# Four x tiles through one DMA queue, and a new emission order for the head of an adaLN attention block

## The chip, the cores and the metric

The kernel runs on one core of a Trainium2 chip. The metric is the device time of one execution in microseconds (us), as a median over several executions. A profiled execution also has a span, from its first to its last recorded instruction, which is a little shorter than its device time. The engines are PE (TensorE: matmuls and transposes), DVE (VectorE), ACT (ScalarE), POOL (GpSimd) and SP (SyncE, here only an issuer of DMAs). Each runs its own instruction stream strictly in order; semaphores tie the streams together.

## The reference, cut to what matters

```python
B, N, D = (2, 256, 1152)
def reference(x, c, wqkv, wo, w_mod):
    mod = (_silu(c) @ w_mod).reshape(B, 6, 1, D)
    shift_a, scale_a, gate_a, shift_m, scale_m, gate_m = [mod[:, i] for i in range(6)]
    h = _layernorm(x, axis=-1) * (1 + scale_a) + shift_a
    q, k, v = split(h @ wqkv)                  # D columns each
    p = _softmax(q @ k.T * D ** (-0.5), axis=-1)
    a = (p @ v) @ wo
    return x + gate_a * a
```

All tensors are bf16. There are 512 tokens (two batches of 256), and the weights are 1152 x 3456 (wqkv), 1152 x 1152 (wo) and 1152 x 6912 (w_mod, of which only the shift, scale and gate thirds of the first half are read).

## The kernel before

**Tiling.** The 512 tokens are four x tiles of 128 tokens: tiles 0 and 1 are batch 0, tiles 2 and 3 are batch 1. The model dimension is nine chunks of 128. Projections keep the activations transposed (feature on partitions): `xnT_sb` holds x transposed, `h0T_sb` (the same buffer as `pvT_sb`) holds it centred and scaled.

**Stages.** The head loads x and c, transposes x on PE, subtracts the token mean and multiplies by 1 + scale. The key projection then accumulates over the nine chunks in seven PSUM banks at once ("ka", `NA` = 7), chunk by chunk as the weights land. Afterwards come two more key blocks, the queries with the shift added, values, scores, softmax, the gate, P times V, the output projection and the stores.

**Loads.** SP issues nearly all loads. First come x tiles 2, 0 and 1, and then the scale columns of w_mod ("s", four groups, into `wm_sb`) alternating with key weight rows ("w", into `wq_sb`), in the order of `LOADS`. Tile 3 and c are issued by ACT, in front of its activation table load. L280 is an x tile, L284 a group of scale columns, L291 a piece of wqkv.

**Emission order.** `ORDER` is a list, written out, of the head's work items; each item appends its instructions to the stream of its engine. So the list fixes the order within each engine, and data dependencies do the rest. `_Prog.op` derives the waits: a read waits for the last writer, and accesses to one PSUM bank by two different engines wait for each other in the order of the list.

The items that the change touches, with their engines and lines:

- `sum i` (ACT, L387): row sums of x tile i, 1.16 us each plus an accumulator read; `sq i` (ACT, L398): row sums of squares. `nmT i` (PE, L363) transposes the sums of a tile into PSUM bank 6. `nmu2` (POOL, L520) turns the sum of tile 2 into a mean that `sq 2` needs.
- `mean 3` (PE, L392): the mean of tile 3 by nine matmuls with ones, from its transposed chunks, also into bank 6.
- `xT i part` (PE, L348): transposes of tile i, part 0 four chunks and part 1 five. `out i part E` (L338 on DVE, L340 on ACT) copies them from PSUM to `xnT_sb`. Tiles 1 and 2 share PSUM banks.
- `nm b E` (L373 on ACT, L371 on DVE): the negative means of batch b from bank 6 to `nm_sb`. `cen cc tiles` (DVE, L382) adds them to a chunk.
- `smm g` (PE, L426): the scale vector of group g, needs load s g; `sev g` (DVE, L456) adds 1 to it. `scale cc tiles E` (L476 on DVE, L480 on ACT) writes `h0T_sb`.
- `early k` and `late k` (PE, L491): the key matmuls of chunk k for five and two of the seven banks.
- `e1`, `d1`, `rc`, `scT`: the small chain ACT, POOL, DVE, POOL that makes silu(c).

After `ORDER`, a fixed program follows: group 2 (chunks 4 and 5) is centred and scaled, then chunks 4 to 8 of the keys run on PE, with `smm 3` (L435, needs the fourth scale load, s3) in front of the last four matmuls of chunk 5.

Of the kernel before, what the change touches and what calls it, by code (L numbers as in the profile page):

```python
# [12 lines left out]
AC = mybir.EngineType.Activation  # L13
POOL = mybir.EngineType.Pool
SP = mybir.EngineType.SP
# [6 lines left out]
class _Prog:  # L22
# [12 lines left out]
    def op(self, eng, fn, r=(), w=(), dma=False, extra=()):  # L35
        o = _Op()
        o.eng, o.fn, o.dma = eng, fn, dma
        o.sem = o.val = None
        o.inc = False
        deps = set(extra)  # L40
        for k in r:
            if k[0] == "ps":
                continue
            p = self.last_w.get(k)
            if p is not None and not (p.eng == eng == PE):
                deps.add(p)
            self.readers.setdefault(k, []).append(o)
        for k in w:
            if k[0] == "ps":
                continue  # L50
            for q in self.readers.get(k, ()):
                if q is not o and (q.dma or dma or q.eng != eng):
                    deps.add(q)
            p = self.last_w.get(k)
            if p is not None and p is not o and not (p.eng == eng == PE):
                deps.add(p)
            self.readers[k] = [o] if k in r else []
            self.last_w[k] = o
        for k in set(r) | set(w):
            if k[0] != "ps":  # L60
                continue
            accesses = self.bank.setdefault(k, {})
            for e, q in accesses.items():
                if e != eng:
                    deps.add(q)
            accesses[eng] = o
        deps.discard(o)
        o.deps = deps
        self.ops.append(o)
        return o  # L70
# [73 lines left out]
D = 1152  # L144
# [22 lines left out]
CUT = ("w", "qa", 8)  # L167
WARM = 5
ORDER = [
    ('cT',), ('warm', 4), ('cTo',), ('sum', 2), ('nmT', 2), ('e1',), ('xT', 2, 0), ('d1',), ('xT', 0, 0),  # L170
    ('xT', 3, 0), ('rc',), ('xT', 3, 1), ('xT', 2, 1), ('sum', 0), ('nmT', 0), ('out', 2, 0, 'D'), ('nmu2',),
    ('out', 3, 0, 'D'), ('scT',), ('sum', 1), ('xT', 1, 0), ('out', 3, 1, 'D'), ('mean', 3), ('out', 0, 0, 'D'),
    ('out', 2, 1, 'D'), ('nm', 1, 'A'), ('xT', 0, 1), ('xT', 1, 1), ('nmT', 1), ('out', 1, 0, 'D'),
    ('out', 1, 1, 'A'), ('cen', 0, (2, 3), 'D'), ('smm', 0), ('cen', 0, (0, 1), 'D'), ('nm', 0, 'A'),
    ('out', 0, 1, 'A'), ('sev', 0), ('scale', 0, (2, 3), 'D'), ('early', 0, (2, 3)), ('scale', 0, (0, 1), 'D'),
    ('cen', 1, (0, 1, 2, 3), 'D'), ('scale', 1, (0, 1), 'D'), ('cen', 3, (0, 1, 2, 3), 'D'),
    ('cen', 2, (0, 1, 2, 3), 'D'), ('early', 0, (0, 1)), ('late', 0), ('scale', 1, (2, 3), 'A'), ('late', 1),
    ('smm', 1), ('sev', 1), ('sum', 3), ('scale', 2, (2, 3), 'A'), ('scale', 2, (0, 1), 'D'), ('early', 1),
    ('sq', 0), ('scale', 3, (0, 1), 'D'), ('late', 2), ('sq', 1), ('scale', 3, (2, 3), 'D'), ('late', 3),
    ('early', 2), ('smm', 2), ('early', 3),  # L180
]

# [1 line left out]
def bass_standalone__dit_adaln_block__diffusion_kernel(  # L184
    nc: bass.Bass,
    x: bass.AP,
    c: bass.AP,
    wqkv: bass.AP,
    wo: bass.AP,
    w_mod: bass.AP,  # L190
    out: bass.AP,
):
    with ExitStack() as es:
        _build(nc, es, x, c, wqkv, wo, w_mod, out)


def _build(nc, es, x, c, wqkv, wo, w_mod, out):
# [81 lines left out]
    def load_x(eng, i):  # L279
        op(eng, lambda e: e.dma_start(x_sb[:, i, :], x_pi[:, i, :]), w=[("x", i)], dma=True)  # L280
# [12 lines left out]

    op(AC, lambda e: e.dma_start(c_sb[:, :], c[:, :]), w=[("c",)], dma=True)
    load_x(SP, 2)
    load_x(AC, 3)
    op(AC, lambda a: a.preload_act_table_set("natural_log_exp_and_others"))
    for t in LOADS:
        pg.tag = ("ld",) + t
# [15 lines left out]
    for k0 in range(0, DC, 3):  # L315
# [7 lines left out]
        out=ident[:, :], in_=ident[:, :], compare_op=ALU.not_equal, fill=1.0,  # L323
# [188 lines left out]
    early, late = tuple(range(EARLY)), tuple(range(EARLY, NA))  # L512
# [332 lines left out]
```

## Time and profile before

| | us |
|---|---|
| median of 4 runs | 97.68 (97.53 to 98.66) |
| profiled execution, its own time | 97.53 |
| profiled execution, its span | 95.7 |
| PE busy | 91.1 |
| DVE, ACT busy | 50.7, 32.1 |

The granted TensorE clock is full over the whole span. When each early load was issued and when it had landed (issue start plus the trace's time from issue to landing):

| load | KB | issued by, at | to landing | landed at |
|---|---|---|---|---|
| x tile 2 | 288 | SP 0.74 | 2.9 | 3.6 |
| x tile 0 | 288 | SP 1.19 | 4.0 | 5.2 |
| x tile 3 | 288 | ACT 1.30 | 5.0 | 6.3 |
| x tile 1 | 288 | SP 1.66 | 4.9 | 6.6 |
| s0 | 576 | SP 2.12 | 6.7 | 8.8 |
| w chunk 0 | 224 | SP 2.60 | 6.8 | 9.4 |
| w chunk 1 | 224 | SP 3.93 | 6.2 | 10.1 |
| s1 | 576 | SP 4.40 | 7.7 | 12.1 |
| w chunks 2, 3 | 448 | SP 5.01 | 8.3 | 13.3 |
| s2 | 576 | SP 7.66 | 7.7 | 15.4 |
| s3 | 864 | SP 10.96 | 8.6 | 19.6 |

To read the profile: a wait is charged to whatever released it, and an engine's idle time costs nothing unless the chain of work that ends last runs through it.

### The profile page before, as it was taken

Reading aid. Unit: us, or ns where it says so; the run is one execution under the profiler, and the core shown is the slowest. Engines: PE = TensorE matmul, PEld = TensorE weight load, DVE = VectorE, ACT = ScalarE, POOL = GpSimd, SP = SyncE. Lnnn points to the kernel's source line nnn. Section 1 sums busy time; section 2 is a strip of 40 time slices with the busy share of each in tenths; the row PEclk is TensorE's granted clock in tenths of the full one; section 3 lists DMA queues with packets and bytes.
Section 4 is the critical chain, followed back from the end, with each engine's and each line's share of the span. In section 5 each row is a group of like instructions: output and inputs, shape, how many; then the busy total and the mean of one; then the engine's idle time right before and its main releaser. Section 6 shows DMA issues by size and latency. Waiting matters only on the chain.

```text
span 95.7 us, 1738 instructions
## 1 busy us (share of the span) xinstructions
PE 91.1 (95%) x705; PEld 50.3 (53%) x705; DVE 50.7 (53%) x130; ACT 32.1 (34%) x66; POOL 1.9 (2%) x12
## 2 busy tenths in 40 slices
PE   5989799999999999999999999999999999999990
PEld 1358555444544454444444486454448765665570
DVE  1049984840549559306602075663308646499971
ACT  2697889976641100005120213335026600000000
POOL 5020000000000000000000000000000000000000
PEclk9999999999999999999999999999999999999999
DMA  2999999999999999999999993111567575712222
GB/s 50 329 335 344 329 313 347 357 318 337 367 368 368 378 338 355 397 388 391 390 392 392 392 323 77 31 27 27 24 27 46 47 45 45 119 65 82 82 82 82
DMA packets 20667, 22.03 MB, mean 230 GB/s; under 512 B 2610, under 2 KB 16690, under 8 KB 20660
## 3 DMA queue, kind: packets, MB, share of 16 engines
q1 hardware_dynamic: 20512, 21.63, 77.9%
q10 hardware_dynamic: 148, 0.30, 1.0%
q8 instruction: 5, 0.08, 0.4%
q14 instruction: 2, 0.02, 0.0%
HBM read 19.76 MB, written 1.18 MB: 219 GB/s over the span
## 4 chain that ended last, share of the span: by engine, by line
PE 77%; SPq 10%; DMA 9%; issue 1%; DVE 0%
PE psbank L491 28%; PE psbank L788 18%; PE psbank L672 16%; DMA wm_sb<-in_w_mod_dram 9%; SPq L291 7%; PE psbank L688 4%; PE psbank L750 4%; PE psbank L659 2%; PE psbank L435 2%; SPq L284 2%; SPq L280 1%; PE psbank L729 1%; PE psbank L414 0%; DVE xo_sb L793 0%
## 5 line engine op out<-in xcount | busy, mean ns | idle before, releaser
L491 PE MATMUL psbank<-pvT_sb,wq_sb 128*128 128x512 bf16 (+1 forms) x86 | 18.7, 367 | 0.6 <-DVE pvT_sb L476 0.6
L491 PE MATMUL psbank<-hT_sb,wq_sb 128*128 128x512 bf16 x81 | 17.8, 379 | 0.0
L788 PE MATMUL psbank<-wm_sb,pvT_sb 128*128 128x384 bf16 x99 | 16.3, 326 | 0.0
L672 PE MATMUL psbank<-wq_sb,hT_sb 128*128 128x512 bf16 x72 | 16.0, 379 | 0.0
L788 PEld LDWEIGHTS psbank<-wm_sb,pvT_sb 128*128 128x128 bf16 x99 | 9.7, 98 | 6.3
L491 PEld LDWEIGHTS psbank<-hT_sb,wq_sb 128*128 128x128 bf16 x81 | 7.8, 98 | 9.5
L491 PEld LDWEIGHTS psbank<-pvT_sb,wq_sb 128*128 128x128 bf16 x86 | 7.9, 98 | 8.5 <-DVE pvT_sb L476 0.7
L340 ACT ACTIVATE qkT_sb<-psbank 128x512 bf16<-128x512 f32 x9 | 5.0, 605 | 19.5 <-PE psbank L491 19.5
L672 PEld LDWEIGHTS psbank<-wq_sb,hT_sb 128*128 128x128 bf16 x72 | 7.0, 98 | 8.3 <-DVE nb_sb L703 0.2
L338 DVE CAST qkT_sb<-psbank 128x512 bf16<-128x512 f32 x9 | 5.7, 683 | 9.2 <-PE psbank L491 9.2
L801 DVE TENSOR_TENSOR ga_sb<-psbank,gate_rep 128x384 bf16<-128x384 f32 x11 | 6.1, 555 | 3.1 <-PE psbank L788 3.0
L682 DVE TENSOR_SCALAR v_sb<-psbank,rstd_sb 128x512 bf16<-128x512 f32 x4 | 3.0, 750 | 8.8 <-PE psbank L672 8.8
L484 DVE SCALAR_TENSOR_TENSOR hT_sb<-std_sb,sh_sb,pvT_sb 128x256 bf16<-128x256 f32 x18 | 7.3, 477 | 0.1
L382 DVE TENSOR_TENSOR xnT_sb<-xnT_sb,nm_sb 128x512 bf16<-128x512 bf16 (+1 forms) x9 | 5.6, 656 | 0.0
L680 ACT ACTIVATE v_sb<-psbank,rstd_sb 128x512 bf16<-128x512 f32 x4 | 2.7, 682 | 7.3 <-PE psbank L672 7.3
L398 ACT ACTIVATE junk_sb<-x_sb,nmu_sb 128x1152 bf16<-128x1152 bf16 x4 | 5.0, 1247 | 0.1
L332 PE MATMUL psbank<-warm_sb 128*128 128x512 bf16 x9 | 3.9, 585 | 1.2 <-DVE warm_sb L319 1.2
L705 ACT ACTIVATE e_sb<-s_sb,nb_sb 128x256 bf16<-128x256 bf16 x4 | 2.0, 507 | 8.2 <-DVE nb_sb L703 8.2
L387 ACT ACTIVATE junk_sb<-x_sb 128x1152 bf16<-128x1152 bf16 x4 | 4.6, 1158 | 0.0
L804 DVE TENSOR_TENSOR xo_sb<-x_sb,ga_sb 128x384 bf16<-128x384 bf16 x11 | 3.9, 358 | 0.4
L688 PE MATMUL psbank<-qkT_sb 128*128 128x256 bf16 x36 | 4.1, 273 | 0.0
L750 PE MATMUL psbank<-pT_sb,v_sb 128*128 128x256 bf16 x36 | 4.1, 273 | 0.0
(72 smaller groups left out, 71.3 us busy)
## 6 DMA issues: line engine op xcount, KB each, us to landing
wq_sb<-in_wqkv_dram SPq DMA_DIRECT2D x3, 864.0 KB, 11.0
wm_sb<-in_w_mod_dram SPq DMA_DIRECT2D x1, 2592.0 KB, 16.1
wm_sb<-in_wo_dram SPq DMA_DIRECT2D x1, 2592.0 KB, 21.8
wq_sb<-in_wqkv_dram SPq DMA_DIRECT2D x4, 448.0 KB, 8.3
wm_sb<-in_w_mod_dram SPq DMA_DIRECT2D x3, 576.0 KB, 7.7
wm_sb<-in_w_mod_dram SPq DMA_DIRECT2D x1, 1440.0 KB, 10.7
wq_sb<-in_wqkv_dram SPq DMA_DIRECT2D x6, 224.0 KB, 6.8
wq_sb<-in_wqkv_dram SPq DMA_DIRECT2D x2, 576.0 KB, 9.9
```

Source lines behind the costliest of these rows:

```text
L291: op(SP, lambda e: e.dma_start(wq_sb[:, k0:k1, c0:c1], wq_v[:, k0:k1, c0:c1]), w=[("w", tag, k) for k in range(k0, k1)], dma=True)
L338: op(DVE, lambda v: v.tensor_copy(dst, src), r=r, w=w)
L340: op(AC, lambda a: a.activation(dst, src, ACT.Copy), r=r, w=w)
L382: op(eng, lambda e: e.tensor_tensor(ap, ap, nm, ALU.add), r=[("xnT", cc, i) for i in tiles] + nk, w=[("xnT", cc, i) for i in tiles])
L398: op(AC, lambda a: a.activation(junk_sb[:, :], x_sb[:, i, :], ACT.Square, bias=nmu_sb[:, i:i + 1], scale=1.0, accum_out=sq_sb[:, i:i + 1]) ...
L484: op(DVE, lambda v: v.scalar_tensor_tensor(hT_sb[:, cc, lo:hi], std_sb[:, lo:hi], sh_sb[:, cc, b:b + 1], h0T_sb[:, cc, lo:hi], op0=ALU.mul ...
L491: op(PE, lambda pe: pe.matmul(ps[bank][:, lo:hi], wq_sb[:, k, col * P:(col + 1) * P], src[:, k, lo:hi], start=(k == 0) if start is None el ...
L672: op(PE, lambda pe, k=k, c0=c0, c1=c1, bank=bank: pe.matmul(ps[bank][:, 0:c1 - c0], hT_sb[:, k, i * P:(i + 1) * P], wq_sb[:, k, 2 * D + c0 ...
L688: op(PE, lambda pe, cc=cc: pe.matmul(ps[bank][:, 0:NTOK], qkT_sb[:, cc, i * P:(i + 1) * P], qkT_sb[:, DC + cc, b * NTOK:(b + 1) * NTOK], s ...
L750: op(PE, lambda pe, h=h, cc=cc, sbk=sbk: pe.matmul(ps[bank][:, h * NTOK:(h + 1) * NTOK], v_sb[:, 2 * b + sbk, cc * P:(cc + 1) * P], pT_sb[ ...
L788: op(PE, lambda pe, i=i, k=k, rhs=rhs, n=n, bank=bank: pe.matmul(ps[bank][:, 0:n], pvT_sb[:, k, i * P:(i + 1) * P], rhs, start=(k == 0), s ...
L801: op(DVE, lambda v, b=b, c0=c0, c1=c1, n=n, bank=bank, s=s: v.tensor_tensor(ga_sb[:, s, 0:n], ps[bank][:, 0:n], gate_rep[:, b, c0:c1], ALU ...
```

## The change

Tile 3 of x is issued by SP, directly after tile 2, instead of by ACT. ACT's queue then holds only the load of c before its table load. SP issues, in turn, tiles 2, 3, 0, 1, then s0, w chunk 0 and so on as before. `ORDER` is replaced: the same items, except that some change engine (`out 1 0` from DVE to ACT; `nm 1`, `scale 1 (2,3)` and `scale 2 (2,3)` from ACT to DVE), in another order. Nothing is added or removed.

```diff
 ORDER = [
-    ('cT',), ('warm', 4), ('cTo',), ('sum', 2), ('nmT', 2), ('e1',), ('xT', 2, 0), ('d1',), ('xT', 0, 0),
-    ('xT', 3, 0), ('rc',), ('xT', 3, 1), ('xT', 2, 1), ('sum', 0), ('nmT', 0), ('out', 2, 0, 'D'), ('nmu2',),
-    ('out', 3, 0, 'D'), ('scT',), ('sum', 1), ('xT', 1, 0), ('out', 3, 1, 'D'), ('mean', 3), ('out', 0, 0, 'D'),
-    ('out', 2, 1, 'D'), ('nm', 1, 'A'), ('xT', 0, 1), ('xT', 1, 1), ('nmT', 1), ('out', 1, 0, 'D'),
-    ('out', 1, 1, 'A'), ('cen', 0, (2, 3), 'D'), ('smm', 0), ('cen', 0, (0, 1), 'D'), ('nm', 0, 'A'),
-    ('out', 0, 1, 'A'), ('sev', 0), ('scale', 0, (2, 3), 'D'), ('early', 0, (2, 3)), ('scale', 0, (0, 1), 'D'),
-    ('cen', 1, (0, 1, 2, 3), 'D'), ('scale', 1, (0, 1), 'D'), ('cen', 3, (0, 1, 2, 3), 'D'),
-    ('cen', 2, (0, 1, 2, 3), 'D'), ('early', 0, (0, 1)), ('late', 0), ('scale', 1, (2, 3), 'A'), ('late', 1),
-    ('smm', 1), ('sev', 1), ('sum', 3), ('scale', 2, (2, 3), 'A'), ('scale', 2, (0, 1), 'D'), ('early', 1),
-    ('sq', 0), ('scale', 3, (0, 1), 'D'), ('late', 2), ('sq', 1), ('scale', 3, (2, 3), 'D'), ('late', 3),
+    ('cT',), ('warm', 4), ('cTo',), ('sum', 2), ('e1',), ('nmT', 2), ('xT', 2, 0), ('xT', 3, 0), ('d1',),
+    ('rc',), ('out', 2, 0, 'D'), ('sum', 0), ('xT', 0, 0), ('xT', 3, 1), ('scT',), ('xT', 2, 1), ('sum', 1),
+    ('out', 3, 0, 'D'), ('nmT', 0), ('out', 3, 1, 'D'), ('xT', 1, 0), ('mean', 3), ('out', 2, 1, 'D'),
+    ('out', 1, 0, 'A'), ('out', 0, 0, 'D'), ('nm', 1, 'D'), ('xT', 0, 1), ('xT', 1, 1), ('nmT', 1), ('smm', 0),
+    ('out', 1, 1, 'A'), ('cen', 0, (2, 3), 'D'), ('cen', 0, (0, 1), 'D'), ('nm', 0, 'A'), ('sev', 0),
+    ('scale', 0, (2, 3), 'D'), ('scale', 0, (0, 1), 'D'), ('out', 0, 1, 'A'), ('cen', 1, (0, 1, 2, 3), 'D'),
+    ('early', 0, (2, 3)), ('early', 0, (0, 1)), ('scale', 1, (2, 3), 'D'), ('scale', 1, (0, 1), 'D'),
+    ('late', 0), ('sum', 3), ('cen', 3, (0, 1, 2, 3), 'D'), ('cen', 2, (0, 1, 2, 3), 'D'), ('late', 1),
+    ('smm', 1), ('sq', 0), ('early', 1), ('sev', 1), ('scale', 3, (0, 1), 'D'), ('scale', 3, (2, 3), 'D'),
+    ('late', 3), ('nmu2',), ('scale', 2, (2, 3), 'D'), ('sq', 1), ('scale', 2, (0, 1), 'D'), ('late', 2),
     ('early', 2), ('smm', 2), ('early', 3),
 ]
...
     op(AC, lambda e: e.dma_start(c_sb[:, :], c[:, :]), w=[("c",)], dma=True)
     load_x(SP, 2)
-    load_x(AC, 3)
+    load_x(SP, 3)
     op(AC, lambda a: a.preload_act_table_set("natural_log_exp_and_others"))
```

## The prediction, made before the changed kernel was run

> **What bounds the kernel now.** I read the chain of waits first, in order of time, because it says which resource the end hangs on at each moment. Columns: start, duration, what.
>
> ```profile
> 0.74 0.39 SPq L280
> ...
> 2.12 0.43 SPq L284
> 2.56 0.04 issue
> 2.60 1.28 SPq L291
> 3.88 0.04 issue
> 3.93 0.43 SPq L291
> ...
> 8.17 2.74 SPq L291
> 10.91 0.04 issue
> 10.96 8.61 DMA wm_sb<-in_w_mod_dram
> 19.56 0.04 issue
> 19.61 0.57 PE psbank L435 x36
> 20.17 0.97 PE psbank L491 x4
> ```
>
> Until 19.6 us the end hangs on loads: SP's issues, then the fourth scale load, s3, which lands at 10.96 + 8.61 = 19.57. From 19.6 on it is PE alone. The second view, busy time by stretch (length, then busy time and count of PE, PEld, DVE, ACT, POOL, then clock, DMA share, GB/s), says how tight each part is:
>
> ```profile
> 2.40:19.60 17.20, 16.13 (x161) 9.15 (x159) 10.50 (x28) 14.71 (x28) 0.64 (x3) 1.00 1.08 336
> 19.60:93.40 73.80, 73.79 (x542) 40.77 (x542) 39.47 (x99) 16.70 (x39) 0.00 (x0) 1.00 0.76 216
> ```
>
> After 19.6 PE is busy 73.79 of 73.80 us. The change touches none of that work, so only the moment at which it starts can move. Before 19.6 the DMA engines are full (share 1.08, packets overlap) at 336 GB/s.
>
> Third, the waits between 10 and 21 us (who waited for whom, total, times, longest) show whether PE or the loads come last:
>
> ```profile
> PEld psbank L491 <- DVE pvT_sb L476: 0.7, 1, 0.7
> PEld psbank L435 <- DMA wm_sb<-in_w_mod_dram: 0.6, 1, 0.6
> ...
> PEld psbank L426 <- DMA wm_sb<-in_w_mod_dram: 0.3, 1, 0.3
> ...
> PE psbank L435 <- DMA wm_sb<-in_w_mod_dram: 0.2, 1, 0.2
> ```
>
> PE twice waits for a load: at `smm 1` until s1 lands at 12.1 (0.34 us in the timeline), and at `smm 3` until s3 lands (0.15 on PE). The L476 row is PE waiting at 10.14 for the first scaled chunk. So PE's head may come 0.34 us later and still meet s1, and 0.34 + 0.15 = 0.49 us later and still meet s3. If it comes earlier, it waits longer for the same two loads. **The head's order is worth little; the landings of s1 and s3 decide.**
>
> **What the Trainium skill says.** "DMA: Bandwidth & Descriptors", section "Issuing engines are not separate DMA queues": DMAs of all issuers run on the same 16 engines and interleave; a second issuer saves only sequencer time. The trace agrees: tile 3, from ACT at 1.30, took 5.0 us to land, tile 1, from SP at 1.66, 4.9, and the engines were then full. The same page, "Queues, rings and completion order": each engine alternates between queues with work. So before, tile 3 shared with tiles 0 and 1; afterwards the four come in line. "TensorE: Matmul & The Clock Gate", Part 1: PE falls to half clock after an idle window of about 3.4 us. PE's longest gap here after 5 us is 0.58, and mine below are shorter than 0.6, so I charge nothing for the clock; no run so far shows a fall.
>
> **The change, part by part.**
>
> *SP's queue.* One more issue of 0.39 to 0.42 us (three x rows: 390 to 424 ns) plus 0.04 between. Tiles 0 and 1, s0 and all that follows on SP come up to 0.46 us later. Is that hidden? The two w loads of 224 KB show it: the first issue took 1.28 us, the next 0.43, the same instruction on the same size. The 0.85 us over is SP held back, and the engines have been full since about 2.4. If what holds it is the drain, the first w issue, starting at 3.06, is released at 3.88 as before, with 0.82 instead of 1.28; the shift ends there. The bytes ahead of s3 are the same and the engines stay full, so s3 lands at 19.6: **cost 0**. The cover is that hold; without it the cost is 0.46. A gain has a ceiling, given below.
>
> *ACT's queue* loses an issue of 0.37 us. The table load, 1.71 to 2.99, comes 0.4 earlier, but ACT then waits 0.88 us for PE until 3.86 anyway: 0.
>
> *x landings.* In line after tile 2 (3.6), the last of the four at 6.6 as before; evenly spaced by (6.6 - 3.6) / 3 = 1.0: tile 3 at 4.6, tile 0 at 5.6, tile 1 at 6.6 (estimates from the landings).
>
> *PE, 5.2 to 8.9.* The order starts with `nmT 2` at 5.25, which waits for `sum 2`, unchanged. Then tile 3's transposes find their data at 5.7, so the idle of 0.35 us at 6.37 (tile 3 landed 6.3) goes; tile 0 comes at about 5.9. On DVE `out 2 0` (0.42, from 5.83), `out 3 0` (0.42), `out 3 1` (0.48) end at 7.2, so `mean 3` starts near 7.2 instead of 7.49. What is late next is ACT: `sum 0` waits for tile 0 and starts at 5.65 instead of 5.30, `sum 1` at 6.95 instead of 6.60, ending 8.2. DVE does `out 2 1` (0.48), `out 0 0` (0.42) and the moved `nm 1` by 8.5; `nmT 1` on PE, which shares bank 6 with it, follows at 8.55 (before: 8.70). `smm 0` then waits for s0 at 8.8: it starts at 8.87 instead of 8.97. All the reordering wins **0.1 us** at this point, because s0's landing comes last.
>
> *DVE, 8.5 to 14.* Chunk 0 is centred in 2 x 0.43 by 9.4, within the wait for `smm 0`; it needs `out 1 0`, moved to ACT behind `sum 1`: 8.15 + 0.61 (nearest row, 605 ns for 512 columns) = 8.8. `nm 1` on DVE: between 0.38 (its ACT row) and 0.43 (DVE's 256 columns with PSUM); I take 0.4. `sev 0` ends at 9.65, first key matmul at 10.05. `scale 1 (2,3)` adds one pitch of 0.21, so centring chunks 3 and 2 ends at 12.61 instead of 12.40; `sev 1` waits for `smm 1` until 12.76 either way, and 0.15 is left. `scale 3` twice and `scale 2` twice end at 13.85 (before three, 13.5). Behind them stand `late 3` and `late 2` on PE, at 12.59 + 5 x 0.227 = 13.7 and 14.2: `scale 3` is done at 13.4 and `scale 2` at 13.85, in time by 0.3. Chunks 4 and 5 are centred by 15.2 instead of 14.84; the next work waited until 16.23 (1.39 us idle, `smm 2`), which covers it. Net on DVE +0.4 + 2 x 0.21 - 0.42 = +0.4 us, all in gaps: 0. If the 0.15 were gone, delay would pass to `late 3` only after 0.3 more.
>
> *ACT* loses those and gains `out 1 0`; `sum 3`, `sq 0`, `sq 1` start about a microsecond earlier (10.5 instead of 11.33), nothing waits for them before 16.5. `nmu2` moves back on POOL; its reader `sq 2` runs at 17.4. `scT` on POOL comes no later than 6.2 and is read at 8.9: 0.
>
> *Sum.* Head -0.1, given back at s1, whose wait grows from 0.34 to 0.44; s1 and s3 unchanged; 73.8 us of PE unchanged. Span 95.7, profiled execution 97.53 + 0 = 97.5. The median stands 0.15 above that execution, so **97.7**, its own range 97.4 to 97.95 (0.3 of landing jitter).
>
> **Rivals.**
>
> *SP's issue is the bound* (slower). The chain runs through SP without a gap until 10.96, and if that is cause and not company, each issue, s3's too, moves by 0.46: s3 lands at 20.0, 97.68 + 0.46 = **98.1**. For it: the unbroken chain. Against it: issues of the same size take 0.43 or 1.28 us. It decides once SP is not held at the first w issue. Joined by a head that has lost over 0.8 us (`sum 0` to `out 1 0` in ACT's queue late by 0.3 of DVE slack plus 0.49 of PE's waits), it would pass the 1% mark: tile 0 would have to land after 7.1 for 0.5 more, **98.6** or above. Nothing in the landings points there.
>
> *The queue gets better* (faster). With one queue s1 and s3 could land earlier, if alternating cost something. PE can use at most the two waits and the 0.1 of its head: 0.34 + 0.15 + 0.1 = 0.59, **97.1**. Against it: the engines were full with both queues.
>
> *The change doesn't do what it says*: if tile 3 still lands at 6.3, its transposes stand ahead of tile 0's in PE's order and hold them for 0.7 us; `out 3 1` ends near 7.4, `mean 3` as before, `smm 0` at 8.97: **97.7** too.
>
> **How the numbers follow.** About 1%, 0.98 us, is what a measurement here can tell from no change. Hidden, including the change that does nothing: 0.66. SP's issue as the bound, 98.1: 0.17, still within 1%. Lost head on top, 98.6 or above: 0.11, of which 0.10 beyond 1%, with what I have mis-sized. Better queue: 0.06, of which 0.03 beyond 1%, by something unseen, since 0.59 is my ceiling. So faster 0.03, same 0.87, slower 0.10. The range runs from 97.2 (most of the faster case) to 98.4 (the SP rival with jitter).
>
> **What would show it.** Right: the first w issue shrinks to about 0.8 us, s3 lands at 19.6, PE's wait at `smm 1` is near 0.44, idle at `smm 3` 0.1 to 0.2, PE full after it. SP rival: the w issues keep 1.28 and 2.6 us and s3 lands at 20.0. Lost head: PE waits on DVE or ACT rows between 10 and 15 us, and no DMA wait is left at `smm 1`. Wrong altogether: s0 landing after 9.3, PE idle beyond 19.6, or a granted clock below 1.

## The result, and the profile after

The changed kernel is slower by about half a percent: ratio to the kernel before 1.0047, 95% interval 1.0027 to 1.0067, from 43 and 64 runs. On the 97.68 us that the prediction started from, that is 98.14 us. (The plain medians, 98.64 and 97.85, also hold disturbed runs, which the ratio leaves out: 12 of the changed kernel's 43 lie above 99.2 us, 8 of these with a granted clock of 0.983, against none of the 64, and why is open.) The profiled execution took 98.91 us, its span is 97.1. It is one sample, and a late one: a second execution of the same program took 98.12.

The chain of waits of the changed kernel, in order of time (start, duration, what), answers to the one shown of before:

```profile
1.66 0.42 SPq L280
2.08 0.04 issue
2.13 0.43 SPq L280
2.56 0.04 issue
2.60 0.43 SPq L284
3.04 0.04 issue
3.08 1.07 SPq L291
4.15 0.04 issue
4.19 0.43 SPq L291
...
9.19 2.66 SPq L291
11.85 0.04 issue
11.90 9.04 DMA wm_sb<-in_w_mod_dram
20.93 0.04 issue
20.98 0.57 PE psbank L435 x36
```

It has the same shape: SP's issues, then the load s3, then PE. s0 is issued at 2.60 instead of 2.12, and the first w issue shrank from 1.28 to 1.07 us, not to the 0.82 of the forecast. s3 is issued at 11.90 instead of 10.96 and lands at 20.93 instead of 19.57. The rest is as full as it was. By stretch (length, busy time and count of PE, PEld, DVE, ACT, POOL, clock, DMA share, GB/s):

```profile
19.60:94.80 75.20, 74.90 (x548) 41.10 (x545) 39.54 (x100) 17.53 (x39) 0.00 (x0) 1.00 0.76 214
```

Of the 0.30 us that PE lacks there, 0.27 lie at the wait for s3. In all fourteen profiled executions of this study, of twelve experiments and the two kernels, the execution's own time is the start of `smm 3` (L435) plus 77.91 to 77.97 us. So only one question is left: what moves the start of `smm 3`?

Where the changed head first differs is ACT, which sums the rows of the x tiles. Its timeline, with the idle time before an instruction in brackets:

```profile
3.94 1.16 ACT L387 ACTIVATE junk_sb<-x_sb 128x1152 bf16<-128x1152 bf16 x1
...
5.64 1.16 ACT L387 ACTIVATE junk_sb<-x_sb 128x1152 bf16<-128x1152 bf16 x1 [0.35 <-DMA x_sb<-in_x_dram]
...
7.89 1.16 ACT L387 ACTIVATE junk_sb<-x_sb 128x1152 bf16<-128x1152 bf16 x1 [0.99 <-DMA x_sb<-in_x_dram]
```

In the kernel before, the sum of tile 1 started without a wait:

```profile
6.60 1.16 ACT L387 ACTIVATE junk_sb<-x_sb 128x1152 bf16<-128x1152 bf16 x1
```

Tile 2 comes as before. Tile 0 is 0.35 us late, as forecast. Tile 1, the last in line, keeps ACT waiting for 0.99 us more: it landed at 7.8, not at 6.6. From there the delay runs on through `nmT 1` (9.35 instead of 8.70) to the first key matmul (11.09 instead of 10.14).

### The profile page after: what moved, and what is told of

Same layout as the page of the kernel before. It is cut to its first block, busy times and chain, and to the rows that moved or that the text cites. A ratio compares the mean times of both kernels' runs of the same rounds, so it can differ in the third digit from the quotient of the medians.

```text
span 97.1 us, 1739 instructions
## 1 busy us (share of the span) xinstructions
PE 92.3 (95%) x705; PEld 51.5 (53%) x705; DVE 51.3 (53%) x132; ACT 31.3 (32%) x64; POOL 1.9 (2%) x12
## 4 chain that ended last, share of the span: by engine, by line
PE 76%; SPq 11%; DMA 9%; issue 1%; DVE 0%
PE psbank L491 28%; PE psbank L788 18%; PE psbank L672 16%; DMA wm_sb<-in_w_mod_dram 9%; SPq L291 8%; PE psbank L688 4%; PE psbank L750 4%; PE psbank L659 2%; PE psbank L435 2%; SPq L280 2%; SPq L284 2%; PE psbank L729 1%; PE psbank L414 0%; DVE xo_sb L793 0%
```

## The experiments

All ratios are to the kernel before, with 95% intervals. Last columns: one profiled execution, in us.

| kernel | ratio | tiles 0, 1 issued | first key matmul | `smm 3` | own time |
|---|---|---|---|---|---|
| before | 1 | 1.19, 1.66 | 10.14 | 19.61 | 97.53 |
| before again | | 1.20, 1.67 | 10.61 | 20.19 | 98.10 |
| new order only | 1.0008 (0.9981 to 1.0035) | 1.19, 1.66 | 10.25 | 19.97 | 97.88 |
| extra issue after s0 | 1.0004 (0.9980 to 1.0028) | as before | 10.51 | 20.66 | 98.57 |
| extra issue late | 0.9992 (0.9961 to 1.0023) | as before | 9.95 | 20.58 | 98.49 |
| extra issue just ahead of s0 | 0.9989 (0.9959 to 1.0020) | as before | 10.20 | 19.65 | 97.56 |
| changed | 1.0047 (1.0027 to 1.0067) | 1.66, 2.13 | 11.09 | 20.98 | 98.91 |
| changed again | | 1.66, 2.71 | 10.34 | 20.21 | 98.12 |
| queue only | 1.0040 (1.0015 to 1.0065) | 1.66, 2.69 | 11.10 | 20.33 | 98.25 |
| extra issue ahead of tiles 0, 1 | 1.0048 (1.0027 to 1.0068) | 1.57, 1.97 | 10.70 | 21.06 | 98.99 |
| three extra issues ahead | 1.0098 (1.0059 to 1.0138) | 2.14, 2.54 | 11.03 | 20.75 | 98.72 |
| tiles 2 and 3 in one load | 1.0096 (1.0059 to 1.0132) | 1.25, 1.76 | 10.69 | 20.27 | 98.18 |
| tile 1 on ACT | 1.0066 (1.0032 to 1.0100) | 1.66, ACT 1.30 | 12.00 | 21.21 | 99.13 |
| tiles 0 and 3 on ACT | 1.0267 (1.0234 to 1.0300) | ACT 1.31, 1.19 | 13.33 | 22.55 | 100.46 |

### The two halves of the change

Queue only:

```diff
-    load_x(AC, 3)
+    load_x(SP, 3)
```

> Tile 3 through SP, with the emission order of before. Three theories. A, SP's issue: every later issue on SP moves by about 0.46 us, so the whole cost of the change, 0.4 to 0.5 us over before, is here. B, landing: with one queue the x tiles and s0 land later (in the changed kernel's profile tile 1 landed at 7.8 instead of 6.6 and s0 at 9.8 instead of 8.8), so the cost is here too, and shows as s0 after 9.3 in the trace; more than with the new order, since the old order waits for tile 0 before tile 3. C, order: the queue costs nothing, within 0.1 us of before, and s0 lands at 8.8 again.

Measured 1.0040. The queue carries the cost, 0.4% of 97.7 being 0.39 us. In its trace SP was held at tile 0, the third x issue, for 1.00 us, so that tile 1 went out 1.03 us later than before and not 0.46. The second trace of the changed kernel has the same hold:

```profile
1.66 1.01 SPq L280
...
2.71 0.43 SPq L280
```

In the first one this issue took 0.42. The prediction had no such hold. New order only:

```diff
-    load_x(SP, 3)
+    load_x(AC, 3)
```

(against the changed kernel)

> The new emission order with tile 3 on ACT as before. A and B: within 0.15 us of before or only what tile 3's late landing at 6.3 costs in an order that wants it at 5.7, which the wait for s0 hides. C, order: 0.4 to 0.5 us slower than before, with PE waiting on DVE or ACT rows between 10 and 15 us.

Measured 1.0008, not to be told from no change. The rewritten order neither costs nor brings anything that shows; theory C falls.

### The issue alone, without the queue

```diff
     load_x(SP, 2)
+    extra_c = op(SP, lambda e: e.dma_start(c2_sb[:, :], c[:, :]), w=[("c2",)], dma=True)
     load_x(AC, 3)
...
-    op(SP, None, extra=outs)
+    op(SP, None, extra=outs + [extra_c])
```

> Before, with one more load on SP directly after x tile 2: c again, 4.5 KB, into a spare buffer. It adds an issue of 0.4 to 0.5 us to SP and hardly any bytes; tile 3 stays on ACT. A, SP's issue: 0.4 to 0.5 us slower, s3 lands at about 20.0 in the trace. B, landing through one queue: within 0.15 us of before, since what the engines carry is the same and the first stretched w issue absorbs the shift. C: within 0.15 us of before.

Measured 1.0048. Tile 3 stays on ACT, the order is the old one, 4.5 KB more are loaded, and the cost is that of the whole change. So it does not take one queue for all tiles (theory B): one more issue in front is enough. Three of them:

> Before, with three small extra loads (c in three pieces) on SP directly after x tile 2, some 1.2 us of issue in all. A, the issue passes straight through to s0, s1 and s3: 1.2 to 1.4 us slower. If there is a slack that a first issue uses up, more than three times the 0.47 of one. If the loss is only a matter of one disturbed start, not of the length: 0.5 us again.

Measured 1.0098. s0 is issued at 3.01 instead of 2.12, tiles 0 and 1 at 2.14 and 2.54 instead of 1.19 and 1.66, each 0.9 us later; the cost, 0.98% of 97.7, is 0.96 us. That is less than the 1.2 to 1.4 expected, because the three small issues moved the tiles by 0.9 us only. The delay passes through at about its own length.

### Where an issue costs nothing

The same extra load was put at three later places in SP's stream. After s0, in front of the first w issue:

```diff
+        if t == ('w', 0, 1):
+            extra_c = op(SP, lambda e: e.dma_start(c2_sb[:, :], c[:, :]), w=[("c2",)], dma=True)
```

> Before, with the same small extra load of c on SP placed after s0, in front of the first w issue. If what counts is the issue of s0 (the head of PE waits for it): no change, within 0.15 us, since s0 is not moved and the first w issue is held anyway. If every issue up to s3 counts: 0.4 to 0.5 us slower, as with the extra load ahead of s0.

Measured 1.0004. SP's timeline there:

```profile
2.13 0.44 SPq L285 DMA_DIRECT2D wm_sb<-in_w_mod_dram  x1
2.61 1.32 SPq L302 DMA_DIRECT2D c_sb<-in_c_dram  x1
3.98 0.96 SPq L292 DMA_DIRECT2D wq_sb<-in_wqkv_dram  x2
```

L302 is the extra load, and it is held for 1.32 us, as the first w issue was before (1.28). A 4.5 KB load takes 0.32 us to issue where SP is free. So in this trace the hold belongs to the place, not to the load. With the condition on `('s', 2)`, after w chunks 2 and 3:

> Before, with the same small extra load on SP after the load of w chunks 2 and 3, where SP is held for over 2 us at each w issue. If SP's holds absorb an issue there, as the prediction said of the first w: no change, within 0.15 us. If SP's chain is the bound even there: 0.4 to 0.5 us slower.

Measured 0.9992. With the condition on `('s', 0)`, between tile 1 and s0:

> Before, with the small extra load of c on SP between x tile 1 and s0: of the loads that the extra one after tile 2 moved, the x tiles now stay where they were and only s0 and what follows it come later, by about 0.4 us. If the issue of s0 carries the cost: 0.3 to 0.5 us slower, as there. If the landing of x tiles 0 and 1 carries it: no change, within 0.15 us.

Measured 0.9989. This is the decisive one. s0 and the first w issue start 0.37 and 0.35 us later. The first w issue then takes 1.03 us instead of 1.28, and what follows up to s1 starts 0.10 later. No loss can be told: the interval ends at 1.0020, and that of the extra issue ahead of tiles 0 and 1 begins at 1.0027. In the trace s0 still lands at 8.9. My reading until then, that s0's issue carries the cost, falls. What the extra issue ahead of tiles 0 and 1 moved, and this one does not, is the issue of tiles 0 and 1. No run has the extra load between the two, so which of them counts is open.

### Taking an issue away again

```diff
-    load_x(SP, 2)
-    load_x(SP, 3)
+    op(SP, lambda e: e.dma_start(x_sb[:, 2:4, :], x_pi[:, 2:4, :]), w=[("x", 2), ("x", 3)], dma=True)
```

> The changed kernel with x tiles 2 and 3 in one load: everything still on SP, new order, but SP has three issues ahead of s0 again, as before the change. A, SP's issue count: the cost goes, within 0.15 us of before, s0 issued near 2.1 and landing at 8.8 to 9.0; up to 0.3 us more if tile 2 landing at 4.3 holds back the sums. B, one queue for all x tiles: still 0.4 to 0.5 us slower than before.

Measured 1.0096, worse, although tiles 0 and 1 are issued only 0.1 us later than before. ACT's timeline shows what the larger load costs:

```profile
4.64 1.16 ACT L386 ACTIVATE junk_sb<-x_sb 128x1152 bf16<-128x1152 bf16 x1 [0.59 <-DMA x_sb<-in_x_dram]
```

Tile 2 now lands with tile 3 at 4.6, and the first sum starts 0.7 us late. The experiment exchanged one late tile for another and cannot tell A from B; its trace (98.18) is also an earlier draw than its median (98.91), so the size is not explained. Tile 1 on ACT:

```diff
     load_x(SP, 3)
+    load_x(AC, 1)
...
-    ('x', 0), ('x', 1), ('s', 0), ('w', 0, 1), ('w', 1, 2), ('s', 1), ('w', 2, 4), ('s', 2), ('w', 4, 6),
+    ('x', 0), ('s', 0), ('w', 0, 1), ('w', 1, 2), ('s', 1), ('w', 2, 4), ('s', 2), ('w', 4, 6),
```

> The changed kernel with x tile 1, not 3, on ACT, and the new order: SP has tiles 2, 3 and 0 ahead of s0, three issues as before the change. If the number of issues ahead of s0 carries the cost: it goes, within 0.15 us of before; faster than before by up to 0.2 if the new order is good for landings in turn. If the order or the single row of x tiles on SP carries it: 0.3 to 0.5 us slower than before.

Measured 1.0066. Three issues ahead of s0 were not enough to take the cost away, but the head was late for a reason of its own, so this run does not test the number of issues. Tile 0, third on SP, landed 6.0 us after its issue, at 7.7, and ACT and PE waited for it:

```profile
7.79 1.16 ACT L388 ACTIVATE junk_sb<-x_sb 128x1152 bf16<-128x1152 bf16 x1 [2.49 <-DMA x_sb<-in_x_dram]
```

And two tiles on ACT, to bring SP forward:

```diff
-    load_x(AC, 3)
+    load_x(AC, 0)
+    load_x(AC, 3)
...
-    ('x', 0), ('x', 1), ('s', 0), ('w', 0, 1), ('w', 1, 2), ('s', 1), ('w', 2, 4), ('s', 2), ('w', 4, 6),
+    ('x', 1), ('s', 0), ('w', 0, 1), ('w', 1, 2), ('s', 1), ('w', 2, 4), ('s', 2), ('w', 4, 6),
```

> Before, with x tile 0 on ACT too, ahead of tile 3: SP issues tiles 2 and 1 and then s0, 0.46 us earlier. A, SP's issue: 0.4 to 0.5 us faster than before (s3 at about 19.1), capped at 0.49 by what PE can use. B: the same as before within 0.2 us, or faster by 0.1 to 0.3 if sharing two queues evenly helps the first landings. C: no change, or slower by 0.2 if tile 3, now second on ACT, comes later for an order made for 6.3.

Measured 1.0267. SP did come 0.46 us earlier, but s0 landed at 8.7 and s3 at 19.6, hardly before the 8.8 and 19.6 of before: in this trace an earlier issue did not bring them forward. Tile 3, second on ACT, landed at 8.3, in company with the loads that SP had issued by then, and PE stood still for it:

```profile
8.33 1.68 PE L349 MATMUL psbank<-ident,x_sb 128*128 128x128 bf16 x14 [2.32 <-DMA x_sb<-in_x_dram]
```

### How far one trace can be trusted

> The kernel before once more, for a second trace: how far do landings scatter between executions of one program? If the single traces can be read for 0.5 us, s0 lands at 8.8 again within 0.15 and s3 at 19.6; the traces of the extra loads after s0 suggest a scatter of 0.4 at s0 and of a microsecond at s3.

> The changed kernel once more, for a second trace: s0 issued at 2.60 again. If s0's issue carries the cost, s0 lands at 9.3 to 9.8 again, later than in both traces of before, and PE reaches the first key matmul at 10.5 or later. If the late landings of the first trace were chance, it lands at 8.8 to 9.0.

The second trace of before has s0 at 9.3 and s3 at 20.15, 0.5 and 0.6 us later than the first; the second of the changed kernel has s0 at 8.9, although it was issued at 3.19 and not at 2.60 again. So the expectation that s0 lands later than in both traces of before failed. The two second traces have s3 at 20.15 and 20.17, no difference at all. A single trace cannot carry a difference of 0.5 us here. The ratios can, and for landings only what all traces of a group share. The six traces with tiles 0 and 1 issued as in the kernel before have `sum 1` starting at 6.51 to 7.32; the five with both tiles later on SP (changed twice, queue only, one and three extra issues ahead) at 7.42 to 7.89, and no value of one group lies in the other, though only 0.10 us parts them.

The same two groups differ in what the DMA engines move between 1.2 and 5.2 us. The four rows below are that stretch (last numbers: DMA share and GB/s) in, first, the kernel before; second, the extra issue just ahead of s0; third, the changed kernel; fourth, the extra issue ahead of tiles 0 and 1:

```profile
1.20:5.20 4.00, 4.00 (x18) 1.31 (x18) 0.07 (x1) 2.62 (x5) 0.88 (x4) 1.00 0.83 270
```

```profile
1.20:5.20 4.00, 4.00 (x18) 1.32 (x18) 0.07 (x1) 2.62 (x5) 0.88 (x4) 1.00 0.85 292
```

```profile
1.20:5.20 4.00, 4.00 (x18) 1.30 (x18) 0.07 (x1) 2.62 (x5) 0.88 (x4) 1.00 0.86 240
```

```profile
1.20:5.20 4.00, 4.00 (x18) 1.32 (x18) 0.07 (x1) 2.62 (x5) 0.88 (x4) 1.00 0.89 248
```

The DMA share is much the same, 0.83 to 0.89, the rate is not. With tiles 0 and 1 issued as before it is 270, 287, 280, 285, 292 and, in the second trace of before, 238; with them later it is 240, 247, 244, 248 and 249. The means, 275 and 246, differ by 29 GB/s, which over 4 us is 0.12 MB, or 0.35 us at the 336 GB/s of the full stretch behind. That is most of the 0.46 us, from single samples of which one falls out of line.

This stretch also holds the start: from 1.2 to 2.4 us the engines of the kernel before are busy for 0.46 and move 104 GB/s. The two groups part later, when the engines are full in both. From 3.6 to 5.2 us, first the kernel before, then the changed kernel:

```profile
3.60:5.20 1.60, 1.60 (x13) 0.57 (x10) 0.00 (x0) 1.34 (x4) 0.00 (x0) 1.00 1.03 390
```

```profile
3.60:5.20 1.60, 1.60 (x13) 0.57 (x10) 0.00 (x0) 1.34 (x4) 0.00 (x0) 1.00 0.98 264
```

Here the first group has 390, 381, 388, 395, 401 and, in the second trace of before, 302; the other has 264, 275, 268, 282 and 286. So the engines do not stand idle. In the changed kernel a byte took about 40% more of their time (0.98 at 264 GB/s against 1.03 at 390).

Nor is the loss over at 5.2 us. Up to there three extra issues lose no more than one (249 GB/s); the rest of their loss comes afterwards. From 5.2 to 9.0 us, the kernel before and the three extra issues:

```profile
5.20:9.00 3.80, 3.45 (x51) 2.91 (x51) 2.82 (x8) 3.10 (x7) 0.64 (x3) 1.00 1.06 336
```

```profile
5.20:9.00 3.80, 3.80 (x44) 3.35 (x42) 2.37 (x7) 2.76 (x6) 0.64 (x3) 1.00 0.89 249
```

Over 1.2 to 9.0 us the six traces of the first group move 295 GB/s in the mean, the four with one issue ahead 275, the one with three 249. At 336 GB/s these gaps are 0.47 and 1.07 us, near the costs of 0.46 and 0.96. The window was chosen after the runs, and each trace is one execution, so this supports the reading and does not prove it.

## Why the prediction was right and where it was wrong

The forecast, no change that can be told and 97.7 us, holds to the percent, and 98.14 lies in the range of 97.2 to 98.4. But the sum said a cost of 0, and measured is 0.46. The range holds the result because it was made wide enough for the rival at 98.1, not because the sum was right. Point by point:

- **Only the start of `smm 3` matters**: right. Own time minus that start is the same to 0.06 us in fourteen executions.
- **The order brings nothing**: right, 1.0008. The 0.1 us that it was to win in the head did not appear at the first key matmul either (10.25 with the new order alone, 10.14 before).
- **A later issue is hidden where SP is held**: right for every issue tried behind the x tiles. Extra issues there cost nothing that can be told at three places (the intervals end at 1.0020 to 1.0028).
- **The same cover for the issue ahead of tiles 0 and 1**: this is the step that failed. The sum took the end of the first w issue as fixed at 3.88 us, and it took busy engines to move the same bytes in the same time. The end moved: the first w issue ran to 4.15 (to 5.27 in the trace of the queue alone), so of 0.48 us only 0.21 were taken up, and later issues lost more. And the engines were as busy from 2.4 us on as the prediction said, before and after, but not at the same rate. The kernel before, then the changed kernel:

```profile
2.40:5.20 2.80, 2.80 (x16) 0.90 (x14) 0.00 (x0) 1.92 (x5) 0.00 (x0) 1.00 0.98 341
```

```profile
2.40:5.20 2.80, 2.80 (x16) 0.89 (x14) 0.00 (x0) 1.53 (x5) 0.00 (x0) 1.00 0.99 301
```

  How this becomes the delay of s3 is not shown. When s3 landed in the trace of the changed kernel, the core had moved 0.30 MB more than when it landed before (20.93 us at 296 GB/s, 19.57 at 301). At 336 GB/s that is 0.9 of the 1.36 us by which it was later there: bytes of other loads had gone ahead of it.
- **The rival with the right size**: SP's issue as the bound, 0.46 and 98.1. Its mechanism was that every issue passes through, s3's too. The extra issues after s0, late, and just ahead of s0 contradict that. Its mechanism holds only for the issues ahead of tiles 0 and 1.
- **x landings evenly spaced at 4.6, 5.6, 6.6**: tiles 3 and 0 came at 4.3 and 5.6, and at 4.6 and 6.0 in the second trace; tile 1, the last, at 7.8 and 6.9. The last in line was later than the even spacing says. The 6.3 at which tile 3 landed from ACT before is a single sample as well: it came at 6.0 in the second trace of before, and at 5.1 to 5.3 in the new order and the three with an extra issue behind the x tiles.
- **0.34 us of PE slack at s1**: misread. The row in the waits was one of PEld; PE itself has no such row, since its matmuls from 10.14 ran on over it. PE's own pace from the first key matmul to `smm 3`, where no load holds it, is 9.22 us (queue only: 20.33 - 11.10 = 9.23; 9.22 and 9.21 with tiles on ACT). Before, 10.14 + 9.22 = 19.36 stood against 19.61. The slack was 0.25 us, not 0.49.

So a late head has two ways to the end, through PE's 9.22 us and through the loads. In both traces of the changed kernel the loads came last (11.09 + 9.22 = 20.31 against 20.98, and 10.34 + 9.22 = 19.56 against 20.21); in the trace of the queue alone PE did. Shown is that delaying tiles 0 and 1 on SP costs what the change costs, and that an extra issue behind them does not. Why busy DMA engines carry less when those two tiles come one issue later stays open. No version here beats the kernel before.

## What to carry to other kernels

Ask of each issue not only whether its queue is held later, but which loads stand behind it: an issue in front of two of the first x tiles was paid in full, the same issue behind them cost nothing that could be told. And do not take a busy share near 1 as a fixed rate: 0.98 went with 341 GB/s here, 0.99 with 301. "DMA: Bandwidth & Descriptors" in the Trainium skill says, in "Issuing engines are not separate DMA queues", that a second issuer saves only issue time; here one issue's time was worth 0.4%, where it lay ahead of tiles 0 and 1. And take slack from the rows of PE, not from those of PEld, whose waits can lie under running matmuls.

## What the runs showed of the hardware

With two tiles on ACT, PE had a gap of 2.32 us, and its clock fell. The stretches of that trace (the number before the last two is the granted clock):

```profile
7.00:8.00 1.00, 0.00 (x0) 0.00 (x0) 0.00 (x0) 0.89 (x2) 0.00 (x0) 0.95 1.05 325
8.00:9.00 1.00, 0.67 (x7) 0.67 (x8) 0.02 (x1) 0.00 (x0) 0.00 (x0) 0.50 1.05 367
...
11.00:12.00 1.00, 1.00 (x16) 0.91 (x14) 0.13 (x2) 0.38 (x1) 0.00 (x0) 0.84 1.07 357
```

From the clocks of these stretches (0.95 and 0.84 at the edges), PE ran at half clock from about 7.9 to 11.3, some 3.4 us. It set in about 1.9 us after PE's last matmul before the gap, and 14 transposes took 1.68 us where the kernel before took 0.95. The Trainium skill's "TensorE: Matmul & The Clock Gate", Part 1, speaks of an idle window of about 3.4 us; in this trace a gap of 2.32 us was enough. The gap of 1.04 us with tile 1 on ACT left the same 14 transposes at 0.95.
